# Mirror images that go from tile to tile, wider runs of u, z loaded once, and a list that reckons transfers by packets

## The chip, the core and the metric

The kernel runs on one core of a Trainium2 chip. Its time is the device time of one execution in microseconds (us). Three runs of the kernel before gave 1464.86 to 1466.71 us, median 1465.71. One more execution was recorded by the hardware profiler; the durations below come from it.

## What is computed

```python
# u, v: (2, 3008, 256); z: (2, 3008, 64)
attn = np.maximum(z @ z.T / S, 0.0) ** 2          # per batch, S = 3008
x    = u * (attn @ v)                             # 6016 tokens x 256
g    = s * np.maximum(x @ w_in1, 0) ** 2 + b      # 256 -> 2048
y    = g @ w_out1                                 # 2048 -> 256
h    = y @ w_in2
out  = (h / (1 + np.exp(-1.702 * h))) @ w_out2
```

The scores are `z @ z.T` with the same z on both sides, so the matrix of scores is symmetric: the block of keys kc and queries c is the mirror image of the block of keys c and queries kc. The weights come as 64-bit floats.

## The kernel before, in words

**Attention.** A batch's 3008 tokens are cut into six chunks, 0 to 5, of 512 tokens (one of 448). For each pair of chunks kc <= c and each of four 128-key steps t, a `Fresh` step (L434) makes scores on TensorE, then on ScalarE a relu, a square and a rounding to fp32r (`hi`); VectorE takes the rest (`lo`), and `add_up` (L412) multiplies v by hi and lo into `accA`. Where kc < c, `turn` (L485) lets VectorE transpose the squared scores in 32x32 blocks into a tile T (128 x 2048, 1 MiB). [...] `park` (L530) writes T to a buffer H in HBM by one DMA (two where c is 5), and `fetch` (L550) reads H into a tile R by four DMAs of 256 KB (six where c is 5), one for each 32 partitions. Later a `Turned` step (L574) casts R to hi (L593, ScalarE), takes lo (L597, VectorE) and multiplies into `accB`. Each batch has fifteen such images. A step's matmuls stand five steps (`LAG`) behind its casts in the list.

**u, z, v.** When a chunk's sum is complete, `gate` (L904) loads u for it with `load_u` (L869): two halves of four DMAs of 64 KB each, in runs of 32 floats (128 bytes), and transposes and multiplies. `load_z` (L306) loads each chunk of z twice, into the lower and the upper 64 partitions, in runs of 128 bytes. `split_v` (L397) splits v into high and low parts.

**Weights and the two layers.** Weights are read as 64-bit words, turned to fp32 on VectorE and ScalarE (`decode`, L645), combined and split (`prepare`, L703) and stored in HBM. This "preparation" is spread over attention (layer 0) and over attention and the first layer (layer 1). The layers multiply pairs of token blocks by eight quads of weights with seven or eight products each; their loads of prepared weights are issued as tiles come free.

**What sets the order.** All work is first put in a list of `Op`s with an engine, a cost and the keys it reads and writes. `ordered` (L25) takes TensorE's list as written (it may reach 16 ahead) and simulates the engines to place everything else; it models the transfers as one pipe at 350 KB per us (`rate`) and never gives a tile out before its pool has one. Pools: 58 cells of 2 KB per partition, 14 "big" of 4 KB, 4 "wide" of 8 KB (T, R and the `up` weights). The program is then emitted in that order. Each engine runs its instructions in order, so a transfer on SyncE's queue (SP) waits behind all issued before it, and a cast of R on ScalarE that waits holds up all of ScalarE.

Of the kernel before, what the change touches and what calls it, by code (L numbers as in the profile page):

```python
# [14 lines left out]
class Op:  # L15


    def __init__(self, engine, cost, late, f, reads, writes, new, adds, free, due, kb, soon):
        self.engine, self.cost, self.late, self.f = engine, cost, late, f
        self.reads, self.writes, self.new, self.adds = list(reads), list(writes), list(new), list(adds)  # L20
        self.free, self.due, self.kb, self.soon = free, due, kb, soon
        self.keys = set(self.reads) | set(self.writes) | set(self.adds)


def ordered(ops, counts, clocks, reach, ahead, bulk, spread, rate):  # L25
# [116 lines left out]
    while len(result) < n:  # L142
# [43 lines left out]
        for j in after[i]:  # L186
            waiting[j] -= 1
            ready[j] = max(ready[j], s0 + (lag(i, j) if not op.kb else op.cost + late))
            if not waiting[j] and ops[j].engine != "PE":
                pending[ops[j].engine].append(j)  # L190
# [4 lines left out]
def attention_mlp_mlp_kernel(  # L195
# [35 lines left out]
    COUNTS = dict(cell=58, big=14, wide=4, ps=4, accA=2, accB=2)  # L231
# [41 lines left out]
    def put(engine, cost, late, f, reads=(), writes=(), new=(), adds=(), free=0, due=None, kb=0, soon=None):  # L273
        ops.append(Op(engine, cost, late, f, reads, writes, new, adds, free, due, kb, soon))
# [7 lines left out]
    def move(kb, f, reads=(), writes=(), new=(), engine="SP", **more):  # L282
        put(engine, 0.45, 2.0, f, reads, writes, new, kb=kb, **more)

    def moves(kb, fs, reads=(), writes=(), new=(), engine="SP", **more):
        def f():
            for g in fs:
                g()

        put(engine, 0.45 * len(fs), 2.0, f, reads, writes, new, kb=kb, **more)  # L290
# [15 lines left out]
    def load_z(bb, t):  # L306
# [8 lines left out]
        for i in range(4):  # L315
# [15 lines left out]
        moves(64 * len(fs["SP"]), fs["SP"], (), [key], [(key, "cell")], due=due)  # L331
        if fs["ACT"]:
            moves(128, fs["ACT"], (), [(key, 1)], (), engine="ACT", due=due)
# [34 lines left out]
    def load_v(bb, c):  # L368
# [24 lines left out]
        moves(128 * len(fs["SP"]), fs["SP"], (), [key], [(key, "big")], due=due)  # L393
        if fs["ACT"]:
            moves(256, fs["ACT"], (), [(key, 1)], (), engine="ACT", due=due)

    def split_v(bb, c, t):  # L397
        raw, key = ("vr", bb, c), ("v", bb, c, t)

        def high():  # L400
            T[key] = cell(f"v_{bb}_{c}_{t}", F32R).rearrange("p (h d) -> p h d", h=2)
            nc.scalar.copy(out=T[key][:, 0, :], in_=T[raw][:, t, :])

        def low():
            w = T[key]
            nc.vector.tensor_tensor(out=w[:, 1, :], in0=T[raw][:, t, :], in1=w[:, 0, :], op=ALU.subtract)
# [166 lines left out]

    class Turned:  # L574
# [70 lines left out]
    def decode(layer, j):  # L645
# [4 lines left out]
        def load(k):  # L650
            if k == 0:
                T[key] = big_tile(f"wr_{layer}_{j}", U32)
                src = w_in[:, j * 2 * P : (j + 1) * 2 * P].rearrange("(k p) f -> p k f", p=P)
                nc.sync.dma_start(out=T[key][:, :CH].rearrange("p (k f) -> p k f", k=2), in_=src)
# [37 lines left out]
        if layer == 0:  # L692
# [8 lines left out]
            vector(HALF, add, [wf] + ([("total",)] if j else []), [("total",)], **more)  # L701

    def prepare(layer, i, with_sums):  # L703
# [64 lines left out]
        for o in range(2):  # L768
# [41 lines left out]
    def load_forms(layer, p, f, some):  # L810
# [12 lines left out]
        move(256, run, [("df", layer, f, i) for i in some], [key], [(key, "cell")])  # L823
# [45 lines left out]
    def load_u(m, h):  # L869
        start, n = tokens(m)  # L870
        key = "ur", m, h
        fs = []
        for i in range(4):

            def f(i=i):
                if key not in T:
                    T[key] = cell(f"ur_{m}_{h}").rearrange("p (t a) -> p t a", a=32)
# [8 lines left out]
        moves(256, fs, (), [key], [(key, "cell")])  # L886

    def turn_u(m, h):
        n = tokens(m)[1]
        ur, ut = ("ur", m, h), ("ut", m, h)  # L890

        def f():
            T[ut] = cell(f"ut_{m}_{h}")
            if m < 2 * LASTC:
                nc.vector.transpose(
                    out=T[ut].rearrange("p (t g a) -> p t g a", t=4, g=4),
                    in_=T[ur].rearrange("p (g t) a -> p t g a", g=4),
                )
            else:
                nc.vector.transpose(out=T[ut][:, :n], in_=T[ur][:, : n // 32, :].rearrange("p t a -> p (t a)"))  # L900

        vector(n, f, [ur], [ut], [(ut, "cell")])

    def gate(m, accs):  # L904
        n, key = tokens(m)[1], ("x", 0, m)
        for h in range(2):
            load_u(m, h)
# [51 lines left out]
    def post(layer, m, h, source, reads):  # L959
# [30 lines left out]
        for i in range(4):  # L990
# [14 lines left out]
            move(64, f, [key], (), (), engine=queue)  # L1005
# [406 lines left out]
    steps = []  # L1412
    groups = [(0, (1, 2, 3)), (1, (2, 3, 4)), (2, (3, 4)), (3, (4,)), (0, (4, 5)), (1, (5,)), (2, (5,)), (3, (5,)), (4, (5,))]
# [12 lines left out]
    def write_list():  # L1426
# [9 lines left out]
        for k in range(len(steps) + LAG):  # L1436
            if k < len(steps):
# [6 lines left out]
                elif t == 0:  # L1444
# [88 lines left out]
        [(20.0, 450.0), (200.0, 800.0)], 350.0,  # L1533
# [45 lines left out]
```

## Time and profile before

| | |
|---|---|
| the profiled execution | 1461.43 us, of which the span is 1459.7 |
| median of the runs | 1465.71 us |
| TensorE busy | 1398.3 us (96%), 6147 matmuls |
| VectorE busy | 1315.0 us (90%) |
| ScalarE busy | 1210.6 us (83%) |
| DMA | 280956 packets, 326.81 MB; 138448 of them under 512 bytes |
| attention | up to about 540 us; after it the two layers |

The rows further down are groups of whole lines. "Busy" is the time in which an engine executes; a matmul takes 0.23 us of TensorE when it runs at full rate. PEclk is the granted clock as a share of full speed; DMA share is the mean busy share of the 16 DMA engines. A number in brackets at a row's end is the idle time of the engine ahead of the instruction, and what ended it. SPq is the queue of DMA issues on SyncE.

### The profile page before, as it was taken

How to read it: one execution, taken by the hardware profiler on the slowest of the kernel's cores; microseconds unless marked ns; L12 is line 12 of the kernel's file. 1: busy time of each engine (PE TensorE's matmuls, PEld its weight loads, DVE VectorE, ACT ScalarE, POOL GpSimd, SP SyncE). 2: the span in 40 equal slices, each digit the busy share in tenths (PEclk: the TensorE clock that was granted, in tenths of full speed). 3: DMA queues.
4: the chain of work that ended last, by engine and by line, in shares of the span. 5: the costliest groups of instructions: out<-in, count | busy, mean ns of one | idle time of the engine just before them, and what ended most of it. 6: DMA issues, size and time to landing. Idle time of an engine off the chain costs nothing.

```text
span 1459.7 us, 20185 instructions
## 1 busy us (share of the span) xinstructions
PE 1398.3 (96%) x6147; PEld 1157.0 (79%) x6147; DVE 1315.0 (90%) x2368; ACT 1210.6 (83%) x2360; POOL 3.0 (0%) x10
## 2 busy tenths in 40 slices
PE   8999897998989879999999999999999999999997
PEld 6877786777878668888887888898888888888896
DVE  7989897788989769999999999989999999999996
ACT  8988786788878559898999989897979797978784
POOL 0000000000000000000000000000000000000000
PEclk9999999999999999999999999999999999999999
DMA  6788999969699988666786847575756665666654
GB/s 160 229 224 262 256 237 205 273 209 248 230 273 262 225 280 278 214 219 223 256 279 203 295 174 242 168 267 168 270 157 240 182 234 162 243 190 228 190 190 108
DMA packets 280956, 326.81 MB, mean 224 GB/s; under 512 B 138448, under 2 KB 210640, under 8 KB 278288
## 3 DMA queue, kind: packets, MB, share of 16 engines
q1 hardware_dynamic: 277056, 324.62, 72.7%
q10 hardware_dynamic: 3664, 0.68, 0.3%
q8 instruction: 48, 0.79, 0.2%
q14 instruction: 60, 0.49, 0.1%
q0 software_dynamic: 128, 0.23, 0.1%
HBM read 245.24 MB, written 80.22 MB: 223 GB/s over the span
## 4 chain that ended last, share of the span: by engine, by line
PE 72%; DMA 9%; DVE 8%; ACT 4%; SPq 4%; issue 2%; ACTq 0%; POOL 0%; DVEq 0%; POOLq 0%
PE ps_d L1048 8%; PE ps_b L1048 8%; PE ps_c L1048 8%; PE accB L1241 7%; PE ps_b L1241 5%; PE ps_a L1048 4%; PE ps_d L1241 4%; DMA R<-H 4%; PE ps_c L1241 3%; PE accA L1241 3%; PE accA L1216 3%; PE accB L1216 3%; PE accA L427 2%; PE accA L422 2%; PE accB L422 2%; PE accA L423 2%
## 5 line engine op out<-in xcount | busy, mean ns | idle before, releaser
L1171 DVE TENSOR_TENSOR lo<-g_c,hi 128x512 fp32r<-128x512 f32 (+1 forms) x540 | 346.8, 678 | 12.3 <-ACT hi L1167 11.7
L1167 ACT CAST hi<-g_c 128x512 fp32r<-128x512 f32 (+1 forms) x540 | 310.5, 617 | 4.1 <-DVE g_c L1156 3.0
L422 PE MATMUL accA<-hi,v 128*128 128x512 f32 (+1 forms) x336 | 132.5, 394 | 8.3 <-ACT hi L462 6.1
L423 PE MATMUL accA<-hi,v 128*128 128x512 f32 (+1 forms) x336 | 130.7, 389 | 0.0
L1048 PE MATMUL ps_d<-op_t,up 128*128 128x512 f32 (+1 forms) x432 | 120.8, 388 | 2.1 <-DVE g_c L1122 1.9
L1048 PE MATMUL ps_b<-op_t,up 128*128 128x512 f32 (+1 forms) x432 | 121.1, 389 | 0.2 <-ACT s_u L1097 0.2
L593 ACT CAST hi<-R 128x512 fp32r<-128x512 f32 x120 | 70.2, 622 | 59.6 <-DMA R<-H 58.5
L422 PE MATMUL accB<-hi,v 128*128 128x512 f32 x240 | 96.4, 402 | 18.8 <-ACT hi L593 18.8
L466 DVE TENSOR_TENSOR lo<-a,hi 128x512 fp32r<-128x512 f32 (+1 forms) x166 | 109.1, 662 | 4.2 <-ACT hi L462 3.8
L1134 ACT ACTIVATE g_c<-g_c 128x512 f32<-128x512 f32 (+1 forms) x144 | 89.6, 623 | 27.9 <-DVE g_c L1122 27.6
L1156 DVE TENSOR_TENSOR g_c<-g_c,g_c 128x512 f32<-128x512 f32 (+1 forms) x156 | 105.7, 677 | 1.5
L455 ACT ACTIVATE a<-ps_s 128x512 f32<-128x512 f32 (+1 forms) x168 | 96.0, 584 | 13.3 <-PE ps_s L451 13.0
L451 PE MATMUL ps_s<-zq,zk 128*128 128x512 f32 (+1 forms) x336 | 98.9, 388 | 8.4 <-ACT a L455 6.4
L427 PE MATMUL accA<-lo,v 128*128 128x512 f32 (+1 forms) x332 | 102.4, 390 | 4.4 <-DVE lo L466 4.4
L458 ACT ACTIVATE a<-a 128x512 f32<-128x512 f32 (+1 forms) x168 | 103.4, 627 | 0.7
L462 ACT CAST hi<-a 128x512 fp32r<-128x512 f32 (+1 forms) x168 | 101.3, 613 | 0.4
L597 DVE TENSOR_TENSOR lo<-R,hi 128x512 fp32r<-128x512 f32 x110 | 71.5, 677 | 30.8 <-ACT hi L593 26.7
L1048 PEld LDWEIGHTS ps_d<-op_t,up 128*128 128x128 f32 x432 | 80.3, 188 | 20.0 <-DVE g_c L1122 4.3
L423 PE MATMUL accB<-hi,v 128*128 128x512 f32 x240 | 95.5, 398 | 0.0
L1241 PE MATMUL accB<-hi,d 128*128 128x512 f32 (+1 forms) x312 | 95.1, 386 | 0.0
L1048 PEld LDWEIGHTS ps_b<-op_t,up 128*128 128x128 f32 x432 | 80.9, 189 | 17.0 <-ACT s_u L1097 0.9
L1137 ACT ACTIVATE g_c<-g_c 128x512 f32<-128x512 f32 (+1 forms) x144 | 88.2, 631 | 0.4
(167 smaller groups left out, 3320.3 us busy)
## 6 DMA issues: line engine op xcount, KB each, us to landing
up<-uf SPq DMA_DIRECT2D x96, 896.0 KB, 4.8
d<-dw SPq DMA_DIRECT2D x114, 256.0 KB, 4.9
R<-H SPq DMA_DIRECT2D x100, 256.0 KB, 6.6
H<-T SPq DMA_DIRECT2D x20, 1024.0 KB, 5.3
d_s<-df1s SPq DMA_DIRECT2D x54, 256.0 KB, 5.8
f<-rows SPq DMA_DIRECT2D x20, 512.0 KB, 6.8
d_s<-df0s SPq DMA_DIRECT2D x72, 128.0 KB, 5.2
d_s<-df0s SPq DMA_DIRECT2D x36, 256.0 KB, 6.0
```

Source lines behind the costliest of these rows:

```text
L422: nc.tensor.matmul(T[k][:, :n], w[:, 0, cols], T[hi][:, :n], **start_flags(k, fresh))
L423: nc.tensor.matmul(T[k][:, :n], w[:, 1, cols], T[hi][:, :n], **start_flags(k, ()))
L427: nc.tensor.matmul(T[k][:, :n], w[:, 0, cols], T[lo][:, :n], **start_flags(k, ()))
L451: nc.tensor.matmul(T[self.p][:, :n], k, T[zq][:, h, :n], start=h == 0, stop=h == 1)
L458: nc.scalar.activation(out=T[self.a][:, :n], in_=T[self.a][:, :n], func=AF.Square)
L462: nc.scalar.copy(out=T[self.hi][:, :n], in_=T[self.a][:, :n])
L466: nc.vector.tensor_tensor(out=T[self.lo][:, :n], in0=T[self.a][:, :n], in1=T[self.hi][:, :n], op=ALU.subtract)
L1048: nc.tensor.matmul(to[:, :n], a[h], y[:, g, :n], start=first and j == 0, stop=False, skip_group_check=True)
L1156: nc.vector.tensor_tensor(out=self.get(to), in0=self.get(x), in1=self.get(y), op=ALU.subtract)
L1167: nc.scalar.copy(out=T[keys[0]][:, :n], in_=self.get(c))
L1171: nc.vector.tensor_tensor(out=T[keys[1]][:, :n], in0=self.get(c), in1=T[keys[0]][:, :n], op=ALU.subtract)
L1241: nc.tensor.matmul(to[:, :n], w[:, h, cols], g[:, :n], start=first and j == 0, stop=False, skip_group_check=True)
```

## The change

`Op` carries `pipe`, the time that a transfer takes of the modelled pipe, worked out by `carry` from its bytes and the length of its runs. FAR holds the eight pairs (kc, c) with c in 1, 2 and 5, which are parked and fetched as before; the seven with c in 3 and 4 go by `send`: sixteen DMAs of 64 KB from T to R, issued as soon as T is complete. Chunks of z other than the first two are loaded for 64 partitions and copied to the other 64 by one DMA inside SBUF. u is loaded by four DMAs of 128 KB in runs of 64 floats; that permutes the 256 columns, so v's columns and the first layer's rows of `w_in` are permuted alike. The second half of `down_whole` is stored only for quads that use it (3 and 7 in layer 0, 7 in layer 1). Pools: 56 cells, 13 big, 5 wide.

```diff
-    COUNTS = dict(cell=58, big=14, wide=4, ps=4, accA=2, accB=2)
+    COUNTS = dict(cell=56, big=13, wide=5, ps=4, accA=2, accB=2)
...
-        if op.kb:
-            pipe = max(pipe, s0 + op.cost) + op.kb / rate
+        if op.pipe:
+            pipe = max(pipe, s0 + op.cost) + op.pipe
...
+    def carry(kb, run):
+        return kb * 1024 / run * (0.0185 + run / 27200) / 16
...
-        for i in range(4):
+        twice = bb == 0 and t < 2
+        for i in range(4 if twice else 2):
...
+        if not twice:
+            move(128, lambda: nc.sync.dma_start(out=T[key][64:], in_=T[key][:64]), [key], [key])
...
-            nc.scalar.copy(out=T[key][:, 0, :], in_=T[raw][:, t, :])
+            nc.scalar.copy(out=permuted(T[key][:, 0, :], "(h i a)"), in_=permuted(T[raw][:, t, :], "(i h a)"))
...
+    def send(bb, kc, c):
...
+        for x in range(4):
+            for g in range(4):
+                def f(x=x, g=g):
+                    src = T[key].rearrange("p b s r -> p b (s r)")[32 * g : 32 * g + 32, x]
+                    nc.sync.dma_start(out=tile_of()[32 * x : 32 * x + 32, g], in_=src)
+                fs.append(f)
+        moves(1024, fs, [key], [to], [(to, "wide")], soon=0.5)
...
-        for o in range(2):
+        for o in range(1 if i in always[layer] else 2):
             store(256, key, ("dw", layer, i, o), lambda to, o=o: nc.sync.dma_start(
...
-    def load_u(m, h):
+    def load_u(m, due):
...
-                    in_=u.rearrange("b s d -> (b s) d")[
-                        start : start + n, h * P + 32 * i : h * P + 32 * i + 32
-                    ].rearrange("(t b) a -> b t a", b=32),
+                    in_=u.rearrange("b s d -> (b s) d")[start : start + n, 64 * i : 64 * i + 64].rearrange(
+                        "(t b) a -> b t a", b=32
+                    ),
...
-        moves(256, fs, (), [key], [(key, "cell")])
+        moves(512, fs, (), [key], [(key, "big")], run=256, due=due)
...
+    FAR = [(kc, c) for c in (1, 2, LASTC) for kc in range(c)]
...
-                    park(bb, kc, c)
+                    (park if (kc, c) in FAR else send)(bb, kc, c)
```

Three places on SyncE's queue show what the new list does. In names, the tile's kind stands first and the last number is a running number; R_1_4 is the image of chunks 1 and 4, ur is u, zr is z, vr is v, H the parked image.

In the second batch, where chunk 4's images are made, this stood before:

```order
L541 DMA H_2_4_4523<-T_2_4_4441 128x2048
L569 DMA R_1_4_4550<-H_1_4_4420 32x4x512 x4
L781 DMA df0s_108<-forms_6_3_4561 128x2x128
L781 DMA df0s_109<-forms_6_3_4561 128x2x128
L781 DMA df0s_110<-forms_6_3_4561 128x2x128
L781 DMA df0s_111<-forms_6_3_4561 128x2x128
L541 DMA H_3_4_4619<-T_3_4_4538 128x2048
L569 DMA R_2_4_4637<-H_2_4_4523 32x4x512 x4
```

At the same place on SyncE's queue stands now:

```order
L601 DMA R_0_4_4299<-T_0_4_4237 32x512 x16
L601 DMA R_1_4_4430<-T_1_4_4372 32x512 x16
L330 DMA zr_5_4547<-in_z_dram 32x14x32
L330 DMA zr_5_4547<-in_z_dram 32x2x32
L330 DMA zr_5_4547<-in_z_dram 32x14x32
L330 DMA zr_5_4547<-in_z_dram 32x2x32
L340 DMA zr_5_4547<-zr_5_4547 64x512
L601 DMA R_2_4_4661<-T_2_4_4463 32x512 x16
```

A write of H and a later fetch behind other transfers became one run of sixteen pieces for each image.

Where chunk 3's images are made in the second batch, SyncE's queue now reads:

```order
L601 DMA R_0_3_3789<-T_0_3_3704 32x512 x16
L601 DMA R_1_3_3877<-T_1_3_3819 32x512 x16
L330 DMA zr_4_3977<-in_z_dram 32x16x32 x2
L601 DMA R_2_3_3986<-T_2_3_3908 32x512 x16
L340 DMA zr_4_3977<-zr_4_3977 64x512
L582 DMA R_1_2_4084<-H_1_2_3575 32x4x512 x4
```

Three sends of 48 pieces now stand right ahead of the fetch of the image of chunks 1 and 2; that fetch stood ahead of all of chunk 3's transfers but one write.

At the end of the second batch's attention, ahead of the last fetch (chunks 4 and 5), SyncE's queue had:

```order
L878 DMA ur_0_5555<-in_u_dram 32x16x32 x4
L878 DMA ur_1_5575<-in_u_dram 32x16x32 x4
L781 DMA df1s_115<-forms_3_3_5313 128x2x128
L781 DMA df1s_116<-forms_3_3_5313 128x2x128
L541 DMA H_4_5_5609<-T_4_5_5483 128x1024
L541 DMA H_4_5_5609<-T_4_5_5483 128x2x384
L790 DMA up_0_1_5627<-uf_76 128x1792
L878 DMA ur_0_5633<-in_u_dram 32x14x32 x4
L820 DMA d_0_s_0_5659<-df0s_111 128x256
L858 DMA rows_5_129<-gx_5562 128x1024
L878 DMA ur_0_5670<-in_u_dram 32x16x32 x4
L569 DMA R_4_5_5697<-H_4_5_5609 32x4x512 x2
```

Now it has there:

```order
L554 DMA H_4_5_5606<-T_4_5_5485 128x1024
L554 DMA H_4_5_5606<-T_4_5_5485 128x2x384
L904 DMA f_0_5618<-rows_0_123 128x1024
L904 DMA f_1_5628<-rows_1_124 128x1024
L808 DMA dw_98<-forms_7_2_5466 128x2x256 x2
L917 DMA ur_5643<-in_u_dram 32x16x64 x4
L829 DMA up_0_1_5670<-uf_76 128x1792
L859 DMA d_0_s_0_5680<-df0s_111 128x256
L842 DMA d_0_0_0_5695<-dw_91 128x512
L582 DMA R_4_5_5727<-H_4_5_5606 32x4x512 x2
```

Sixteen issues of u around the last image became four; the rest of u stands earlier, or behind the fetch, and two loads of the first layer's operands (f) moved in.

## Rows read from the trace of the kernel before

**Rows 1.** Busy time by stretch; the first line names the columns; stretches of each phase

```profile
core 0: us, PE busy (x) PEld busy (x) DVE busy (x) ACT busy (x) POOL busy (x), PEclk, DMA share, GB/s
0.00:540.00 540.00, 490.56 (x2104) 400.69 (x2105) 454.77 (x918) 425.64 (x851) 0.34 (x6) 0.96 0.87 238
600.00:850.00 250.00, 249.00 (x1089) 203.25 (x1088) 247.36 (x429) 228.90 (x437) 0.00 (x0) 1.00 0.68 231
850.00:900.00 50.00, 49.92 (x220) 40.65 (x219) 44.64 (x73) 46.13 (x89) 0.00 (x0) 1.00 0.61 211
1200.00:1250.00 50.00, 50.00 (x221) 41.12 (x220) 47.33 (x79) 38.74 (x73) 0.00 (x0) 1.00 0.70 215
```

**Rows 2.** The same view of attention's stretches where TensorE falls behind

```profile
0.00:20.00 20.00, 14.49 (x54) 8.80 (x55) 12.17 (x25) 15.26 (x30) 0.34 (x6) 1.00 0.76 171
140.00:160.00 20.00, 13.31 (x52) 10.14 (x51) 14.96 (x26) 13.48 (x27) 0.00 (x0) 0.83 1.01 268
230.00:260.00 30.00, 22.13 (x83) 16.37 (x83) 24.47 (x49) 22.49 (x46) 0.00 (x0) 0.89 0.93 240
270.00:280.00 10.00, 8.86 (x37) 6.40 (x36) 5.93 (x12) 8.24 (x16) 0.00 (x0) 1.00 0.85 252
290.00:300.00 10.00, 4.66 (x12) 3.26 (x13) 6.37 (x12) 7.32 (x15) 0.00 (x0) 0.71 0.55 151
350.00:360.00 10.00, 5.20 (x16) 3.71 (x16) 7.17 (x14) 5.72 (x12) 0.00 (x0) 0.83 1.03 278
410.00:420.00 10.00, 6.10 (x22) 4.76 (x21) 6.22 (x12) 6.53 (x13) 0.00 (x0) 0.83 1.08 300
480.00:530.00 50.00, 38.17 (x150) 30.29 (x149) 35.44 (x68) 26.57 (x52) 0.00 (x0) 0.86 0.98 265
```

**Rows 3.** Who waited for whom: total us, times, longest us

```profile
ACT hi L593 <- DMA R<-H: 58.5, 13, 7.2
PE accB L422 <- ACT hi L593: 18.8, 4, 6.5
```

**Rows 4.** Timeline of ScalarE: start, length, casts of R that waited for it

```profile
150.70 0.62 ACT L593 CAST hi<-R 128x512 fp32r<-128x512 f32 x1 [6.52 <-DMA R<-H]
...
248.50 1.66 ACT L593 CAST hi<-R 128x512 fp32r<-128x512 f32 x3 [3.76 <-DMA R<-H]
...
292.68 0.62 ACT L593 CAST hi<-R 128x512 fp32r<-128x512 f32 x1 [5.49 <-DMA R<-H]
...
355.38 2.18 ACT L593 CAST hi<-R 128x512 fp32r<-128x512 f32 x4 [4.25 <-DMA R<-H]
...
413.47 1.66 ACT L593 CAST hi<-R 128x512 fp32r<-128x512 f32 x3 [5.05 <-DMA R<-H]
...
517.27 2.18 ACT L593 CAST hi<-R 128x512 fp32r<-128x512 f32 x4 [7.16 <-DMA R<-H]
```

**Rows 5.** DMA issues: count, KB each, median us from issue to landing

```profile
R<-H SPq DMA_DIRECT2D x100, 256.0 KB, 6.6
H<-T SPq DMA_DIRECT2D x20, 1024.0 KB, 5.3
...
ur<-in_u_dram SPq DMA_DIRECT2D x80, 64.0 KB, 2.7
```

**Rows 6.** Length of one issue on SyncE, ns min/median/max, fetches and u

```profile
L569 SPq DMA_DIRECT2D R<-H x140: 302/431/3325, 30.5 to 512.3; - x140
...
L878 SPq DMA_DIRECT2D ur<-in_u_dram x96: 311/487/2129, 193.5 to 533.0; - x96
```

**Rows 7.** Timeline of SyncE's queue: two of the loads of u late in attention

```profile
471.81 6.98 SPq L878 DMA_DIRECT2D ur<-in_u_dram  x8
...
481.11 4.68 SPq L878 DMA_DIRECT2D ur<-in_u_dram  x8
```

**Rows 8.** DMA queues: packets, MB, share of 16 engines' span; the queue of small packets

```profile
q10 hardware_dynamic: 3664, 0.68, 0.3%
```

**Rows 9.** One instruction of the preparation on VectorE, ns min/median/max

```profile
L673 DVE SCALAR_TENSOR_TENSOR mt<-wr,mt x32: 648/688/700, 15.4 to 788.9; 128x512 f32<-128x512 uint32 x32
```

More of the change, by code (lines that the diff above doesn't have):

```diff
@@ L15, with __init__, ordered @@
 class Op:
-    def __init__(self, engine, cost, late, f, reads, writes, new, adds, free, due, kb, soon):
+    def __init__(self, engine, cost, late, f, reads, writes, new, adds, free, due, pipe, soon):
         self.engine, self.cost, self.late, self.f = engine, cost, late, f
         self.reads, self.writes, self.new, self.adds = list(reads), list(writes), list(new), list(adds)
-        self.free, self.due, self.kb, self.soon = free, due, kb, soon
+        self.free, self.due, self.pipe, self.soon = free, due, pipe, soon
         self.keys = set(self.reads) | set(self.writes) | set(self.adds)
-def ordered(ops, counts, clocks, reach, ahead, bulk, spread, rate):
+def ordered(ops, counts, clocks, reach, ahead, bulk, spread):
     n = len(ops)
@@ L271, in attention_mlp_mlp_kernel, with put @@
     ops, T = [], {}
-    def put(engine, cost, late, f, reads=(), writes=(), new=(), adds=(), free=0, due=None, kb=0, soon=None):
-        ops.append(Op(engine, cost, late, f, reads, writes, new, adds, free, due, kb, soon))
+    def put(engine, cost, late, f, reads=(), writes=(), new=(), adds=(), free=0, due=None, pipe=0, soon=None):
+        ops.append(Op(engine, cost, late, f, reads, writes, new, adds, free, due, pipe, soon))
     def scalar(n, f, reads=(), writes=(), new=(), **more):
@@ L280, in vector, with move, moves @@
         put("DVE", 0.065 + (0.00056 if fast else 0.00105) * n, 0.14, f, reads, writes, new, **more)
-    def move(kb, f, reads=(), writes=(), new=(), engine="SP", **more):
-        put(engine, 0.45, 2.0, f, reads, writes, new, kb=kb, **more)
-    def moves(kb, fs, reads=(), writes=(), new=(), engine="SP", **more):
+    def carry(kb, run):
+        return kb * 1024 / run * (0.0185 + run / 27200) / 16
+    def move(kb, f, reads=(), writes=(), new=(), engine="SP", run=2048, **more):
+        put(engine, 0.45, 2.0, f, reads, writes, new, pipe=carry(kb, run), **more)
+    def moves(kb, fs, reads=(), writes=(), new=(), engine="SP", run=2048, **more):
         def f():
@@ L288, in f @@
                 g()
-        put(engine, 0.45 * len(fs), 2.0, f, reads, writes, new, kb=kb, **more)
+        put(engine, 0.45 * len(fs), 2.0, f, reads, writes, new, pipe=carry(kb, run), **more)
     def matmuls(count, n, f, reads=(), adds=(), writes=(), new=()):
@@ L392, in load_v, with permuted @@
         due = 0.5 if (bb, c) == (0, 0) else None
-        moves(128 * len(fs["SP"]), fs["SP"], (), [key], [(key, "big")], due=due)
+        moves(128 * len(fs["SP"]), fs["SP"], (), [key], [(key, "big")], run=1024, due=due)
         if fs["ACT"]:
-            moves(256, fs["ACT"], (), [(key, 1)], (), engine="ACT", due=due)
+            moves(256, fs["ACT"], (), [(key, 1)], (), engine="ACT", run=1024, due=due)
+    def permuted(x, order):
+        return x.rearrange(f"p {order} -> p h i a", h=2, i=4)
     def split_v(bb, c, t):
@@ L652, in load @@
                 T[key] = big_tile(f"wr_{layer}_{j}", U32)
-                src = w_in[:, j * 2 * P : (j + 1) * 2 * P].rearrange("(k p) f -> p k f", p=P)
-                nc.sync.dma_start(out=T[key][:, :CH].rearrange("p (k f) -> p k f", k=2), in_=src)
+                to, src = T[key][:, :CH].rearrange("p (k f) -> p k f", k=2), w_in[:, j * 2 * P : (j + 1) * 2 * P]
+                if layer:
+                    nc.sync.dma_start(out=to, in_=src.rearrange("(k p) f -> p k f", p=P))
+                    return
+                for h in range(2):
+                    half = src.rearrange("(i h a) f -> h i a f", i=4, h=2)[h]
+                    nc.sync.dma_start(out=to[:, h], in_=half)
             else:
@@ L701, in decode @@
             vector(HALF, add, [wf] + ([("total",)] if j else []), [("total",)], **more)
+    always = [set(range(NQ)).intersection(*[SEVEN.get((layer, p), ()) for p in range(NP)]) for layer in range(2)]
     def prepare(layer, i, with_sums):
@@ L821, in run @@
                 T[key, i] = t[:, y].rearrange("p (h n) -> p h n", h=2)
-        move(256, run, [("df", layer, f, i) for i in some], [key], [(key, "cell")])
+        move(128 * len(some), run, [("df", layer, f, i) for i in some], [key], [(key, "cell")], run=1024)
         for i in some:
@@ L1003, in f @@
                 )
-            move(64, f, [key], (), (), engine=queue)
+            move(64, f, [key], (), (), engine=queue, run=128)
     form_key = {}
```

39 lines of the change are left out of this document (27 added, 12 removed).

## The prediction

> **What bounds the kernel now.** I read the busy time by stretches first. After 600 us TensorE is busy for 249.0 of 250 us and later for all of 50, at a granted clock of 1.00 [rows 1]: the two layers run at TensorE's rate, and nothing that this change does can shorten them. In the 540 us before, TensorE starts 2104 matmuls. At the rate of the later stretch (221 in 50 us, 4.42 per us, 0.226 us each) it could start 2387. The 283 that are missing are 64 us: all that can be won lies there, and the kernel keeps some 1396 us whatever is done.
>
> Next I cut attention finely. The missing matmuls sit in a few stretches [rows 2]: 4.42 times the length, less the matmuls started, times 0.226 us. The start, 0 to 20: 34, 7.8 us. 140 to 160: 36, 8.2 us. 230 to 260: 50, 11.2. 270 to 280: 7, 1.6. 290 to 300: 32, 7.3. 350 to 360: 28, 6.4. 410 to 420: 22, 5.0. 480 to 530: 71, 16.1. Without the start that is 55.8 us. Each price holds the idle time and the slow clock behind it: the granted clock is 0.71 to 0.89 in those stretches whose TensorE stood longest, and 1.00 in the layers [rows 1, 2].
>
> Then who waits. ScalarE waited 13 times, 58.5 us in total, for a transfer from H to R, and TensorE then for ScalarE's cast of R [rows 3]. The timeline puts these waits at the stretches above: 6.5 us ahead of 150.7, 3.8 ahead of 248.5, 5.5 ahead of 292.7, 4.3 ahead of 355.4, 5.1 ahead of 413.5, 7.2 ahead of 517.3 [rows 4]. By SyncE's order the casts at 150.7, 355.4 and 413.5 are of images (1,4) of the first batch, (0,3) and (1,4) of the second; all three go by send now. The casts at 248.5, 292.7 and 517.3 are of (4,5) of the first batch, (0,1) and (4,5) of the second; these are parked and fetched as before. The DMA engines are 87% busy over attention and at 0.93 to 1.08 in most of the bad stretches [rows 1, 2]: the images are late because the pipe and SyncE's queue are full.
>
> **Sends.** An image was a write (5.3 us to landing), then four fetches (6.6 us each, issued 0.43 us apart), with other transfers between [rows 5, 6]: 5.3 + 4 x 0.43 + 6.6 = 13.6 us with nothing between. Now it is sixteen pieces of 64 KB. The trace has no copy from SBUF to SBUF. Below, 16 x 0.43 + 2.7 (the landing of a 64 KB load of u) = 9.6 us; above, at the price of u under load (8 in 6.98 us, 0.87 each [rows 7]), 16 x 0.87 + 2.7 = 16.6 us. I take 9.6 to 11, nearest to the fetch, whose runs are as long (2 KB) where u's are 128 bytes. The room for it I counted in ScalarE's order, from the square of an image's last step to the first cast of R; one ScalarE instruction passes each 0.63 us in attention (540 / 851 [rows 1]). The three images above have 31, 29 and 30 instructions now (37, 40 and 40 before): 18 us, of which the transposition takes some 3. So 15 us hold 9.6 to 11, and hold nearly the upper bound. I give these stretches back for 85%: 0.85 x 19.6 = 16.7 us.
>
> **Less on the pipe.** Fourteen sends save one megabyte each, 14.7 MB. Attention moves 238 GB/s at 87% busy, 274 GB/s of full pipe, so that is 54 us of it. u keeps its bytes and has 24,064 packets instead of 48,128, z 14,336 instead of 24,576. A small packet costs up to 19 ns of an engine: 0.3% of 16 x 1459.7 us over 3664 [rows 8]; below, nothing, if only bytes counted. So up to 34,304 x 19 ns / 16 = 41 us more. Together 54 to 95 of 470 busy us.
>
> **The end of attention, 480 to 530.** u's bursts go (two of eight issues took SyncE 7.0 and 4.7 us [rows 7]), and of the sixteen issues around the last image four are left. The room of the last four images, (1,5) to (4,5), grows from 38, 29, 27 and 28 instructions to 42, 40, 38 and 38: ten more are 6.3 us, against a longest wait of 7.2 [rows 4]. But f and prepared weights, some 3.3 MB by the shapes in the order against 2.0, now stand between the last write and its fetch. I take 75%: 12 us of 16.1.
>
> **230 to 260.** Images (3,5) and (4,5) of the first batch have 29 and 34 instructions for 26 and 32: one or two us more, against waits of up to 4.5. u and z around them halve their issues. Half: 5.5 of 11.2.
>
> **270 to 300.** The room of (0,1) stays at 39. The eight loads of u right ahead of its write go, the write of weights among them stays. Half: 4.5 of 8.9.
>
> **What is added.** Issues: a send has sixteen for five, u four for eight, z three for four; SyncE gets about 90 more, 39 us at 0.43 [rows 6], in a queue that waits much. Where three sends stand together and the fetch of (1,2) right behind them, 48 issues take 20.6 us or more; that fetch has about 93 to 99 instructions of room from its square, but only a few from its own issue. Between nothing (LAG covers five steps of TensorE) and a full wait of 7 us in each batch; I take 2 each, 4 in all. Preparation: by VectorE's order two more of the 64-bit blocks (five instructions each), 5 more splits and 8 more sums of layer 1 now stand behind attention. These 23 are at most 0.69 us each [rows 9], 15.9 us; the splits and sums cover 128 to 512 columns where that one covers 512, so I take 10. VectorE is busy for 247 of 250 us in the first layer up to 850 and 44.6 of 50 behind [rows 1]. TensorE lost 1 us there with one quad of weights for each pair of blocks, and now a fourth pair gets one: 1 us, between 0 (44.6 + 5 still fits) and 5 (half of it late). The permuted copies of v, the strided transposes of u, the split load of `w_in` and the smaller pools keep elements and instructions nearly as they were; 0, within 1 us either way, behind ScalarE's and VectorE's idle time in attention. The start keeps its 7.8 us.
>
> **The sum.** 16.7 + 12 + 5.5 + 4.5 - 4 - 1 = 33.7 us less. The profiled execution took 1461.4 (a span of 1459.7 and 1.7 around it), so 1427.7 for its like; the median of the runs lies 4.3 above it, which gives 1432.
>
> **Rivals.** First, the fetched images stay as late as they are: six of the sixteen remaining fetches have the room they had, to within two instructions, and the pipe is still some 75% busy. Only the sends' 16.7 us less 5 come: 1454. For it speaks that a fetch with room for 39 instructions was late by 5.5 us at 292.7, when the DMA share was only 0.55 [rows 2, 4], so fullness of the pipe isn't all. Against it, the room grows by ten at the end. Second, nearly everything goes: 55.8 less 4, 1414. For it, late images are the cause of most waits [rows 3]; against it, VectorE is busy for 455 of 540 us [rows 1] and has less slack in 505. Third, slower: SyncE's queue becomes what is late. Its place is the sends of chunks 3 and 4, its price the piece. At 0.43 us the 224 pieces take 96 us of the queue; each 0.1 us more adds 22. If half of that shows (five of seven sends have short room, and hold up what stands behind them), the gain of 33.7 is gone at 0.30 more, so it decides from 0.73 us a piece. At u's 0.87 the half is 49 us, and the time 1481. u's rows under a full pipe say 0.59 to 0.87 [rows 7]; against it, u's runs are 128 bytes. The Trainium skill (SBUF — State Buffer, Can I just issue two DMAs to hit both halves?) has a rule against this change: two concurrent DMAs, on tiles at partition 0 and at 64, gained 6% over one, so they serialize. Pieces that follow one another at the landing of u's would take 16 x 2.7 = 43 us a send. The trace speaks against it: eight issues of u pass in 4.68 us with a landing of 2.7 each, so several are under way at once [rows 5, 7]. Fourth, images come in time and TensorE waits for VectorE or `up` weights instead: no change, 1465.
>
> **How the numbers follow.** The forecast has 52%, the first and the second rival 17% each, the third 8%, the fourth 6%. Faster (by over 0.2%, 3 us, about what a measurement of this kernel can tell from none): 86%. Same: 6%. Slower: 8%. The forecast's own range, with sends at 50 to 100% and the fetches at 30 to 80% of their losses, is 1422 to 1450 (20.7 to 48.6 us won, less 5). For 8 times in 10 it must take in the second rival and the first: 1410 to 1462.
>
> **What would show it.** In the new profile ScalarE's waits for transfers from T to R should be under 5 us in total, those from H to R about 20. An issue of a send should last 0.4 to 0.5 us. 480 to 530, shifted by what was won before, should start over 200 matmuls. The DMA share of attention should be near 0.76, packets some 36,000 fewer. The stretch of the first layer should stay within 2 us of TensorE's rate. I'm wrong if sends last over 12 us, if the fetch of (1,2) makes TensorE wait over 4 us in a batch, or if attention ends at the same time with the images in time.

## The result and the profile after

The changed kernel takes 1475.7 us (median of 4 runs, 1472.7 to 1477.2), the kernel before 1465.3 beside it: the ratio is 1.0067, 95% interval 1.005 to 1.0085. It is slower by 0.7%, where 1432 us and a gain were forecast. The profiled execution took 1477.2 us, its span is 1475.4.

I start with the windows. Columns as in [rows 1, 2]: busy us and, in brackets, instructions of TensorE, its weight loads, VectorE, ScalarE and GpSimd; then the granted clock, the DMA share and GB/s. First the kernel before, cut at 560 us, by which attention is over, in two stretches in which it had lost next to nothing, and in two whose rows are wanted below:

```profile
0.00:560.00 560.00, 509.18 (x2185) 415.26 (x2186) 473.89 (x952) 443.24 (x885) 0.34 (x6) 0.96 0.86 239
560.00:1459.70 899.70, 889.14 (x3964) 741.78 (x3962) 841.12 (x1416) 767.32 (x1476) 2.63 (x4) 1.00 0.66 215
100.00:120.00 20.00, 19.52 (x86) 16.15 (x87) 19.93 (x46) 15.22 (x30) 0.00 (x0) 1.00 0.60 191
360.00:390.00 30.00, 30.00 (x134) 24.83 (x133) 27.45 (x59) 25.11 (x50) 0.00 (x0) 1.00 0.50 169
...
270.00:300.00 30.00, 23.28 (x91) 17.40 (x90) 22.00 (x42) 22.75 (x46) 0.00 (x0) 0.90 0.77 216
530.00:550.00 20.00, 18.72 (x83) 15.15 (x82) 16.09 (x27) 15.36 (x29) 0.00 (x0) 1.00 0.76 252
```

The same of the changed kernel, with the stretches of [rows 2] behind them:

```profile
0.00:560.00 560.00, 508.12 (x2133) 411.01 (x2134) 449.82 (x904) 431.64 (x857) 0.34 (x6) 0.95 0.72 197
560.00:1475.40 915.40, 903.58 (x4016) 748.25 (x4014) 862.79 (x1465) 782.22 (x1504) 2.62 (x4) 1.00 0.67 217
100.00:120.00 20.00, 11.05 (x32) 7.73 (x31) 8.96 (x16) 6.20 (x13) 0.00 (x0) 0.66 0.78 203
360.00:390.00 30.00, 18.65 (x69) 14.05 (x68) 12.92 (x22) 14.60 (x29) 0.00 (x0) 0.77 0.75 187
...
140.00:160.00 20.00, 15.59 (x66) 12.31 (x65) 13.62 (x26) 13.38 (x29) 0.00 (x0) 0.93 0.64 188
230.00:260.00 30.00, 27.88 (x123) 21.84 (x122) 27.13 (x53) 22.57 (x46) 0.00 (x0) 1.00 0.99 252
270.00:300.00 30.00, 30.00 (x127) 24.64 (x126) 25.10 (x47) 28.29 (x58) 0.00 (x0) 0.95 0.76 228
350.00:360.00 10.00, 10.00 (x46) 8.29 (x45) 8.10 (x16) 9.46 (x20) 0.00 (x0) 1.00 0.39 94
410.00:420.00 10.00, 10.00 (x46) 8.29 (x45) 9.11 (x21) 10.00 (x22) 0.00 (x0) 1.00 0.42 99
480.00:530.00 50.00, 46.23 (x199) 39.32 (x200) 47.33 (x99) 40.23 (x80) 0.00 (x0) 0.93 1.04 292
530.00:550.00 20.00, 15.90 (x59) 11.74 (x58) 12.26 (x20) 10.72 (x20) 0.00 (x0) 0.91 1.05 317
```

By 560 us TensorE has started 52 matmuls fewer: 52 x 0.227 = 11.8 us. Behind it 4016 matmuls take 915.4 us, where the rate of before (3964 in 899.7) would take 911.5: 3.9 us. Together that is the 15.7 us between the spans. The old bad stretches of [rows 2] start 193 matmuls more than before. New bad ones have come; the two largest are 100 to 120 and 360 to 390, with 54 and 65 matmuls fewer, 27 us, and in them the granted clock is 0.66 and 0.77, where it was 1.00.

They are not the whole loss. In a kernel that runs behind or ahead, a window by the clock holds other work than before, so the same place in the work has to be compared too. Each trace has 6147 matmuls of TensorE; the table sets the start of the n-th beside that of the n-th before (the two orders differ by a few places), both counted from the first matmul. The last column is of a run below.

| matmul | starts before at, us from the span's start | the change lags by, us | send_4_same_order lags by, us |
|---|---|---|---|
| 100 | 30.5 | 2.6 | 2.4 |
| 400 | 101.5 | -0.4 | -0.7 |
| 450 | 112.9 | 12.7 | -0.7 |
| 550 | 135.6 | 12.7 | -0.7 |
| 600 | 155.5 | 11.4 | -9.4 |
| 700 | 177.4 | 11.4 | -9.4 |
| 950 | 231.3 | 16.6 | -9.5 |
| 1000 | 251.2 | 10.9 | -17.8 |
| 1050 | 265.4 | 15.2 | -14.2 |
| 1200 | 309.7 | 4.8 | -24.6 |
| 1350 | 343.7 | 6.9 | -23.6 |
| 1400 | 361.6 | 0.3 | -30.2 |
| 1450 | 373.0 | 15.2 | -30.2 |
| 1600 | 407.0 | 15.2 | -30.2 |
| 1650 | 423.8 | 10.3 | -35.6 |
| 1750 | 445.6 | 10.3 | -35.7 |
| 1850 | 466.9 | 22.4 | -35.7 |
| 2050 | 527.8 | 6.5 | -48.5 |
| 2100 | 539.1 | 13.4 | -41.1 |
| 2250 | 574.9 | 11.4 | -43.1 |
| last | 1450.3 | 15.4 | -38.8 |

The two large stretches lose 13.1 us (matmuls 400 to 450) and 14.9 (1400 to 1450) by this count. Two others lose 5.2 (700 to 950) and 12.1 (1750 to 1850), and smaller ones 4.3 (1000 to 1050) and 6.9 (2050 to 2100).

The timeline of SyncE's queue (start, length, line, instruction, count) shows what stands at the two largest, and two sends between them:

```profile
72.00 10.65 SPq L601 DMA_DIRECT2D R<-T  x16
82.75 1.09 SPq L330 DMA_DIRECT2D zr<-in_z_dram  x2
83.94 21.49 SPq L601 DMA_DIRECT2D R<-T  x32
105.47 0.59 SPq L340 DMA_DIRECT2D zr<-zr  x1
106.16 1.97 SPq L582 DMA_DIRECT2D R<-H  x4
...
143.02 12.12 SPq L601 DMA_DIRECT2D R<-T  x16
...
179.90 10.01 SPq L601 DMA_DIRECT2D R<-T  x16
...
362.21 10.01 SPq L601 DMA_DIRECT2D R<-T  x16
372.27 0.59 SPq L340 DMA_DIRECT2D zr<-zr  x1
372.90 2.02 SPq L582 DMA_DIRECT2D R<-H  x4
```

From 72 to 105 us SyncE issues almost nothing but the 48 pieces of three sends, 0.63 to 0.67 us each. Behind them stand the copy of chunk 4's z (L340) and the fetch of the image of (1,2); the expectations below call an image a half. The timelines of the engines that want them (the idle time before, and its releaser, in brackets):

```profile
107.85 0.71 DVE L348 STREAM_TRANSPOSE zt<-zr 128x512 f32<-128x512 f32 x1 [9.16 <-DMA zr<-zr]
...
109.52 0.80 PE L464 MATMUL ps_s<-zq,zk 128*128 128x512 f32 x1 [6.44 <-DVE zq L361]
...
113.80 2.18 ACT L625 CAST hi<-R 128x512 fp32r<-128x512 f32 x4 [13.83 <-DMA R<-H]
...
156.81 0.62 ACT L625 CAST hi<-R 128x512 fp32r<-128x512 f32 x1 [6.62 <-DMA R<-T]
...
191.42 0.62 ACT L625 CAST hi<-R 128x512 fp32r<-128x512 f32 x1 [7.30 <-DMA R<-T]
```

Waits up to 560 us (total, times, longest), against [rows 3]:

```profile
ACT hi L625 <- DMA R<-H: 40.8, 8, 15.3
DVE zt L348 <- DMA zr<-zr: 22.7, 4, 9.2
ACT hi L625 <- DMA R<-T: 20.8, 6, 7.3
PE ps_s L464 <- DVE zq L361: 15.1, 3, 8.0
```

The casts' waits, 40.8 us for fetched images and 20.8 for sent ones, come to 61.6 us, for 58.5 before.

And the length of one issue in ns (min/median/max), against [rows 6]:

```profile
L601 SPq DMA_DIRECT2D R<-T x224: 507/589/1906, 72.0 to 448.7; - x112
...
L582 SPq DMA_DIRECT2D R<-H x84: 302/430/1682, 33.4 to 526.2; - x84
```

### The profile page after: what moved, and what is told of

Read it like the earlier page. It is cut to its first block, busy times and chain, and to the rows that moved or that the text cites. A ratio compares the mean times of both kernels' runs of the same rounds, so it can differ in the third digit from the quotient of the medians.

```text
span 1475.4 us, 20284 instructions
## 1 busy us (share of the span) xinstructions
PE 1411.7 (96%) x6147; PEld 1159.3 (79%) x6147; DVE 1312.6 (89%) x2368; ACT 1213.9 (82%) x2360; POOL 3.0 (0%) x10
## 2 busy tenths in 40 slices
DMA packets 243309, 308.73 MB, mean 209 GB/s; under 512 B 105280, under 2 KB 174144, under 8 KB 242432
## 4 chain that ended last, share of the span: by engine, by line
PE 56%; DMA 15%; DVE 11%; SPq 9%; ACT 7%; issue 3%; ACTq 0%; POOL 0%; DVEq 0%; POOLq 0%
PE ps_b L1093 8%; PE ps_d L1093 8%; PE ps_c L1093 8%; SPq L601 7%; PE accB L1286 6%; PE ps_d L1286 4%; PE ps_a L1093 4%; PE ps_b L1286 4%; DMA wr<-in_moe_w_out_dram 4%; DMA R<-H 3%; PE accA L1286 3%; PE ps_c L1286 3%; PE accA L1261 2%; DVE lo L1216 2%; PE accB L1261 2%
## 5 line engine op out<-in xcount | busy, mean ns | idle before, releaser
L625 ACT CAST hi<-R 128x512 fp32r<-128x512 f32 x120 | 70.2, 619 | 67.4 <-DMA R<-H 40.8
L464 PE MATMUL ps_s<-zq,zk 128*128 128x512 f32 (+1 forms) x336 | 105.2, 401 | 17.5 <-DVE zq L361 15.1
L479 DVE TENSOR_TENSOR lo<-a,hi 128x512 fp32r<-128x512 f32 (+1 forms) x166 | 108.5, 657 | 13.1 <-ACT hi L475 12.6
L1179 ACT ACTIVATE g_c<-g_c 128x512 f32<-128x512 f32 (+1 forms) x144 | 89.4, 621 | 32.8 <-DVE g_c L1167 32.5
L440 PE MATMUL accA<-lo,v 128*128 128x512 f32 (+1 forms) x332 | 105.1, 399 | 10.9 <-DVE lo L479 10.9
L464 PEld LDWEIGHTS ps_s<-zq,zk 128*128 128x128 f32 x336 | 65.6, 197 | 34.4 <-DVE zq L361 15.3
```

What stands on the lines that cost most here:

```text
L440: nc.tensor.matmul(T[k][:, :n], w[:, 0, cols], T[lo][:, :n], **start_flags(k, ()))
L464: nc.tensor.matmul(T[self.p][:, :n], k, T[zq][:, h, :n], start=h == 0, stop=h == 1)
L479: nc.vector.tensor_tensor(out=T[self.lo][:, :n], in0=T[self.a][:, :n], in1=T[self.hi][:, :n], op=ALU.subtract)
```

## The experiments

My theory after this: SyncE's queue works in order, a piece takes 0.6 to 0.7 us of it, and what stands behind the sends comes late. Rivals: A, the copy of z in itself; B, the list's new order and prices; C, the transfer from tile to tile in itself. Ratios are to the kernel before (1460 to 1463 us beside these runs); differences between kernels that were measured at different times are taken from the ratios, 0.1% being 1.46 us.

**The parts of the change, taken away or moved one by one**

```diff
 z_twice:    -twice = bb == 0 and t < 2
             +twice = True
 piece_price: the list's price of a sent piece 0.45 -> 0.65
 no_sends:   -FAR = [(kc, c) for c in (1, 2, LASTC) for kc in range(c)]
             +FAR = [(kc, c) for c in range(1, NCH) for kc in range(c)]
 sends_pool: in send(), nc.sync.dma_start -> nc.gpsimd.dma_start, engine="POOL"
```

> All of z is loaded twice from memory, so no half of it is copied from tile to tile; the sends stay as they are. Theory (the sends fill SyncE's queue at 0.6 to 0.7 us a piece, and whatever stands behind them is late, above all chunk 4's z copy and the fetch of the half of (1,2)): zt's longest waits for z (9.2 us, twice) fall under 2 us, but the casts still wait some 13 to 15 us for the half of (1,2), so that the windows 100 to 120 and 360 to 380 gain only some 3 to 5 us each; 1464 to 1471 us. Rival A (the copy of z by itself, a second transfer in series, is what was lost): both windows fill, and the time falls by 20 us or more, under 1456. Rival B (the list's new order and prices, whatever is moved): no change, 1473 to 1478.

Measured 1481.8 us, 1.0131 (1.0102 to 1.0159). Slower than the change by some 9 us, which none of the three expected. Rival A falls: without any copy, three sends still stand ahead of the fetch of (1,2), and in the first batch TensorE waits 9.4 us for its cast, at 113.4. So the late fetch alone is enough there.

> Only the list's price of a sent piece is changed, from 0.45 to 0.65 us, which is near what SyncE takes for one; the instructions are the same, their order is made anew. Theory: the list now sees the queue as it is, puts the copy of z and the fetch of (1,2) ahead of some of the pieces or sends later; the waits of 9 us for z and of 14 to 15 us for the half of (1,2) become less than half, 1455 to 1466 us. Rival A: as far as the copy of z comes earlier the same, else nothing. Rival C (the transfer from tile to tile is slow in itself, not its issue): the images sent are as late as before and the time stays at 1470 to 1480.

Measured 1481.2 us, 1.0128 (1.0111 to 1.0146). My theory's number was wrong: told the price, the list put 48 pieces in one run of 31.7 us instead of moving anything past them. By its number rival C (1470 to 1480) came nearest, but since the new order did not let anything past the pieces, that neither helps nor hurts it.

> All fifteen halves are written to memory and fetched back, as in the kernel before; longer runs of u, the single load of z and the list's reckoning by packets stay. Theory (the sends are what is lost): no queue of 48 pieces, the copy of z lands in time, and the time is that of the kernel before or a little under it, 1458 to 1467 us. Rival A (the copy of z in itself): still 1470 or more, with zt waiting some 9 us for z. Rival B (the list's order and prices): 1470 or more, with z in time but images late at other places.

Measured 1434.9 us, 0.9812 (0.9792 to 0.9833). Without the sends the rest of the change gains 28 us on the kernel before, more than the theory expected (1458 to 1467 us); the sends cost 2.55%, 37 us. The copy of chunk 4's z goes out at 84.98 instead of 105.47, and the fetch behind it does not stand behind pieces:

```profile
84.98 0.53 SPq L340 DMA_DIRECT2D zr<-zr  x1
...
87.45 2.69 SPq L582 DMA_DIRECT2D R<-H  x4
```

> The 224 pieces are issued by GpSimd on its own queue instead of SyncE's, and the list reckons them there. Theory (SyncE's queue is what delays the copy of z and the fetch of (1,2)): SyncE is free, z's waits fall under 3 us and those for the half of (1,2) under 6 us, 1445 to 1462 us, unless GpSimd takes far longer for a piece than SyncE does. Rival C (the transfer from tile to tile is slow in itself): casts wait for the images sent as much as now or more (20.8 us in all now), 1470 or more. Rival A: as far as the copy of z comes early, some 20 us.

Measured 1446.9 us, 0.9892 (0.9876 to 0.9907): 26 us better than the change, as the theory has it, but 12 worse than no sends. The casts still wait 21.5 us for the images sent, as much as in the change (20.8), which the expectation had named as rival C's sign; what went is the wait for z and for (1,2). A piece takes GpSimd 0.496 us (median of 224), and then VectorE waits to write the next T until the old one is sent:

```profile
DVE T L508 <- DMA R<-T: 22.0, 4, 7.1
```

**From the kernel without sends: pieces, u, z, prices**

```diff
 fetch_16:      the seven halves' fetch, per 32 rows x 4 groups -> per 32 rows x 1 group
 ns_u_narrow:   load_u, turn_u, split_v and the load of w_in as in the kernel before
 ns_z_twice:    twice = True
 ns_flat_price: -return kb * 1024 / run * (0.0185 + run / 27200) / 16
                +return kb / 350.0
```

> From no_sends (all halves by memory, 1434.9 us): the seven halves that the change sends are fetched from memory in 16 pieces of 64 KB instead of 4 of 256 KB, same bytes, same packets of 2 KB, 168 more instructions on SyncE's queue, which the list prices at 0.45 us as it does a sent piece. Theory (the number of instructions on SyncE's in-order queue is the loss): 168 x 0.43 us = 72 us more of the queue, in runs of 7 us beside the copy of z and the next fetches; at least a third of the 41 us that the sends cost comes back, 1448 to 1476 us. Rival C (the transfer from tile to tile is the loss): the same as no_sends, 1432 to 1440.

Measured 1461.0 us, 0.9987 (0.9972 to 1.0003), 26 us slower than no_sends without any image sent from tile to tile. Against rival C; but the order is new too, so the 26 us are not yet the price of the instructions alone.

> From no_sends: u is again loaded in runs of 128 bytes by halves into small tiles, without permuted columns of v and w_in. It tells what of the 28 us that no_sends gains on the kernel before is u's. By packets: 16,384 more packets of some 0.023 us over 16 engines, some 24 us of the pipe in an attention whose DMA share is 0.9 already. Theory (pipe relief by u and z is the gain): 1445 to 1458 us. Rival (the list's reckoning by packets is the gain): 1432 to 1440.

Measured 1446.4 us, 0.9884 (0.9863 to 0.9906), 11 us slower than no_sends. The packets are 24,961 more (267,596 for 242,635), not 16,384.

> From no_sends: all of z loaded twice from memory again, no copy from tile to tile. Some 18,000 more packets of 128 bytes, some 26 us of the pipe, against one copy in series for each chunk. Theory (pipe relief): slower by 3 to 15 us, 1438 to 1450. Rival A (the copy in series costs something everywhere): faster, 1425 to 1433.

Measured 1420.7 us, 0.9704 (0.9684 to 0.9725): 16 us faster than no_sends, on the side of rival A, and 43 us faster than the kernel before. It is the fastest of all runs. The packets are 9,825 more (252,460), not 18,000, so the theory's 26 us of the pipe were nearly twice too many.

> From no_sends: the list reckons a transfer again by its size alone (1 us for 350 KB) instead of by packets; the transfers are the same, only their order is made with the old price. Theory (pipe relief is the gain, the reckoning little): within 6 us of no_sends, 1429 to 1441. Rival (the reckoning is the gain): 1450 or more.

Measured 1455.8 us, 0.9948 (0.9931 to 0.9966): 20 us slower, as the rival expected (1450 or more).

**Is the reckoning a gain of its own, and how much is mere order?**

```diff
 before_packets: the kernel before, +carry()'s reckoning with each transfer's run length
 z_on_pool:      the change, the copy zr<-zr by nc.gpsimd on its queue
 sends_pool_zt:  sends_pool and z_twice together
 ns_zt_nudge, after_nudge, before_nudge:
                 the list's price of each issue 0.45 -> 0.46
```

> The kernel before with one thing changed: its list reckons a transfer by its packets (packets of 0.0185 us + run length / 27,200, over 16 engines) instead of by size. No transfer changes, only the order. Theory (ns_flat_price lost 21 us, so the reckoning is worth about that much by itself): 1438 to 1452 us. Rival (the reckoning helps only with the shorter pipe of wide u and single z): 1456 or more.

Measured 1443.5 us, 0.9888 (0.9873 to 0.9903): 16 us faster than the kernel before.

> The changed kernel with the copy of z from tile to tile issued by GpSimd, whose queue is empty, instead of by SyncE behind the sends. Theory (two losses of 12.5 and 14.4 us begin where chunk 4's copy stands behind up to three sends, but the fetch of the half of (1,2) stands there too and stays late): zt's waits of 9.2 us go, casts wait as now (40.8 us), and 4 to 16 us come back, 1459 to 1472. If the copy alone decided (rival A), 20 us or more come back, under 1456.

Measured 1467.9 us, 1.0053 (1.0037 to 1.007). Some 2 us better than the change by the ratios, which their intervals do not tell from none, and less than I expected; the list placed two loads of z and the fetch of (1,2) behind the pieces again.

> The sends issued by GpSimd, and all z loaded twice without a copy from tile to tile: every other part of the change as it is. It shows what sends are worth once SyncE's queue is spared, against the same kernel without sends (1420.7 us). Theory (a send of 16 pieces on any one queue takes 8 to 10 us and lands later than the park and fetch that it replaces): slower than that, 1425 to 1447 us. Rival (sends are good where the queue is free, since they spare a way to memory and back): 1405 to 1420.

Measured 1436.7 us, 0.984 (0.9825 to 0.9854): 20 us slower than ns_z_twice, as the theory has it.

> A control: the kernel without sends and without the copy of z (1420.7 us), in which the list prices each issue at 0.46 instead of 0.45 us. Nothing else changes but what order follows from that. How far the time moves is how far a mere change of order moves it: 1415 to 1430 us if the differences of 11 us and more between these kernels come from what was changed in them; 1435 or more if they are the order's luck.

Measured 1434.6 us, 0.9826 (0.9811 to 0.984): 18 us slower than ns_z_twice from a change of order alone, practically at the bound that I had set for luck. So the 11 us of u, the 16 us of z and the 12 us between sends_pool and no_sends can't be told from it; the 16 and 20 us of the reckoning and the 20 us of sends_pool_zt hardly, and sends_pool_zt lies within 2 us of this control.

**The same order, another number of instructions**

That left open whether 37 us, and the 26 of fetch_16, were order too. In the next two every engine's order stays as it is, and the number of pieces into which a transfer is cut changes.

```diff
 send_4_same_order, from the change; the list still reckons 16 pieces:
-  for x in range(4):
-      for g in range(4):
-          ... [32 * g : 32 * g + 32, x]  ->  tile_of()[32 * x : 32 * x + 32, g]
+  for x in range(4):
+      ... [32 * x : 32 * x + 32]  ->  tile_of()[32 * x : 32 * x + 32]
 fetch_16_same_order, from no_sends: as fetch_16; the list still reckons 4 pieces
```

> The changed kernel with every engine's work in exactly the changed kernel's order, but each send is 4 pieces of 256 KB instead of 16 of 64 KB: same bytes from tile to tile, 168 instructions fewer on SyncE's queue. It leaves out that the blocks change places, so what it sends is not the mirror image. Theory (the number of instructions on the in-order queue is the loss): a send takes some 2 us of the queue instead of 10, chunk 4's copy of z and the half of (1,2) come in time, and 20 to 40 of the 41 us come back, 1436 to 1456 us. Rival C (the transfer from tile to tile, or when it lands): 1466 or more. Rival (the list's order with sends in it is simply bad): 1460 or more too, with SyncE free.

Measured 1422.6 us, 0.9731 (0.9702 to 0.9759): 3.4% or 49 us faster than the change, more than I expected. SyncE's queue, the casts' waits for fetched images and the window up to 560 us:

```profile
71.65 3.37 SPq L600 DMA_DIRECT2D R<-T  x4
75.13 2.25 SPq L330 DMA_DIRECT2D zr<-in_z_dram  x2
78.05 10.76 SPq L600 DMA_DIRECT2D R<-T  x8
88.86 1.12 SPq L340 DMA_DIRECT2D zr<-zr  x1
90.07 2.50 SPq L582 DMA_DIRECT2D R<-H  x4
```

```profile
ACT hi L624 <- DMA R<-H: 10.8, 7, 4.4
```

```profile
0.00:560.00 560.00, 543.81 (x2375) 448.32 (x2376) 502.69 (x996) 483.43 (x956) 0.34 (x6) 0.98 0.82 225
```

The copy of z goes out 16.6 us earlier, the casts' waits for fetched images fall from 40.8 to 10.8 us, and 242 more matmuls start by 560 us. In the table above the change's four largest losses, 45.3 us together, are gone (matmuls 400 to 450, 700 to 950, 1400 to 1450, 1750 to 1850). The small ones at the start, from 1000 to 1050 and from 2050 to 2100 stay, so the sixteen pieces did not make them. The transfers are still from tile to tile, still a megabyte each: rival C falls, and with it rival B, since the order is the changed kernel's own. One thing differs besides the count: a piece's runs are 8 KB long here, not 2, so part of the 49 us may belong to that.

> The kernel without sends (1434.9 us) with every engine's work in exactly its order, but the seven halves fetched in 16 pieces instead of 4 (the list still reckons 4). Theory: 168 instructions of some 0.42 us, 70 us of the queue, cost 10 us or more without any change of order, 1445 to 1475 us. Rival (the 26 us that the 16 pieces cost before were the luck of a new order): 1432 to 1441.

Measured 1474.8 us, 1.009 (1.0056 to 1.0124), 2.8% or 41 us slower than no_sends. Here bytes and runs are the same, so this is the cleanest of the runs: 168 instructions more bring 2690 packets (242,635 to 245,325, some 16 each, nearly all under 512 bytes) and 0.02 MB. Its waits look like the change's, z's too, and two images' fetches hold SyncE for 16 us:

```profile
ACT hi L627 <- DMA R<-H: 43.1, 11, 10.3
...
DVE zt L353 <- DMA zr<-zr: 12.7, 2, 6.4
```

```profile
349.29 16.18 SPq L584 DMA_DIRECT2D R<-H  x32
...
365.98 0.52 SPq L340 DMA_DIRECT2D zr<-zr  x1
```

With each matmul set beside the same one of no_sends, all of the 41 us are lost within attention.

> A control: the changed kernel, in which the list prices each issue at 0.46 instead of 0.45 us. The work is the same, its order is made anew. If the loss against the kernel before belongs to the sends, 1465 to 1485 us; if it was one unlucky order, under 1455.

Measured 1474.0 us, 1.0081 (1.0052 to 1.011): the loss is not one unlucky order. With z_twice, piece_price and z_on_pool, five orders with the pieces on SyncE's queue lie at 1.0053 to 1.0131; three with neither sends nor sixteen pieces and with wide u and the reckoning by packets at 0.9704 to 0.9826.

> A control: the kernel before, in which the list prices each issue at 0.46 instead of 0.45 us. Order alone moved a kernel without sends by 14 us; so I expect within 15 us of the kernel before, 1446 to 1476. Outside that, the comparison of before and after says little about the change.

Measured 1458.3 us, 0.9965 (0.995 to 0.998): 5 us, inside what I expected. The kernel before is not one lucky order.

## Why the prediction was wrong

The step that failed most is "What is added". It said: "SyncE gets about 90 more, 39 us at 0.43 [rows 6], in a queue that waits much", "48 issues take 20.6 us or more", and then "I take 2 each, 4 in all". Measured: the 48 pieces and two loads of z took 33.4 us (72.00 to 105.43), and the two stretches behind such runs cost 28 us, not 4 (27 by the clock). Two errors made that. The piece was sized by the fetch, 0.43 us, and takes 0.589 at the median and 0.67 in a run. And I counted only the fetch of (1,2) as waiting behind the sends, with 93 to 99 instructions of room; the second thing there, chunk 4's copy of z, had no term in the sum at all. It is on TensorE's path by zt and zq: 15.1 us of its waits, up to 8.0 each. For the cast of (1,2) TensorE waited only 2.1 and 3.0 us more behind that; but z_twice shows that the fetch alone would have held it as long.

The second step that failed is "Sends", by the same wrong price. Together the two make 45 of the 49 us between the forecast (33.7 us less) and the result (15.7 more): 24 by "What is added", 21 by "Sends". send_4_same_order shows that cutting a send into sixteen made both. Step by step, by the table of matmuls:

- Sends: their three stretches gained 1.3, 6.6 and 4.9 us (matmuls 550 to 600, 1350 to 1400, 1600 to 1650), 12.8 for 16.7. But 17.3 us were lost in two places that had no term, 700 to 950 and 1750 to 1850, and with four pieces a send both losses are gone. By the order in which chunk 4's images are sent, the late ones in the first batch are (1,4), one of the three whose room I had counted, and (3,4), whose room I had not: the casts wait 6.6 us at 156.8, where (1,4) had waited 6.5 before, and 7.3 at 191.4. From the first issue to the cast these took 13.8 and 11.5 us, for "9.6 to 11"; the issue alone is 10.0 to 12.1. In the second batch two casts wait 2.7 and 3.4 us (437.7 and 450.8). Casts wait 20.8 us for sends in all, for "under 5".
- Less on the pipe: right. 280,956 packets became 243,309, 37,647 fewer for "some 36,000", and the DMA share up to 560 us fell from 0.86 to 0.72, for 0.76. That it did not help says that the pipe was not what was late: no_sends has 0.87 up to 560 us and is 37 us faster, and in the sends the share is 0.39 to 0.42 at 94 to 99 GB/s (350 to 360, 410 to 420). A piece of 64 KB each 0.67 us is 98 GB/s; with the pipe under half busy, I take it that the queue sets that rate.
- The end of attention: about as forecast, 15.9 us (1850 to 2050) for 12, though part of that makes good what 1750 to 1850 had lost. Just behind it, 2050 to 2100, 6.9 us are lost. send_4_same_order loses 7.4 there, so the sixteen pieces did not make it, and the cause stays open.
- 230 to 260 and 270 to 300: 11.8 us (950 to 1200) for 10.
- The layers: 4.0 us (2250 to the last) for 1, within the 0 to 5 given. VectorE is busy 862.8 of 915.4 us behind 560 us, for 841.1 of 899.7; that more of the preparation fell behind attention than I had counted would explain it, and is not shown.
- The smaller things, "0, within 1 us": not settled. u's narrow loads cost 11 us in one order, the single load of z 16 in another, and order alone 18. The list's reckoning by packets, which I gave no term, came out at 16 and 20 us in two comparisons. No more can be said of the parts' own sizes.

The third rival had the mechanism, the place and nearly the time (1481 for 1475.7), and I gave it 8%. That the time lay so near is partly luck: it was worked out for 0.87 us a piece, and at 0.67 the same rule gives 27 us, 1459. I set its threshold at 0.73 us a piece, reckoning that half of a longer issue would show. Runs at 0.67 already sufficed, since in fetch_16_same_order even a median of 0.42 us a piece costs 41 us: what matters, as I read it, is that 16 instructions stand in a row ahead of others, not their last tenth. I let "nearest to the fetch" decide a price whose upper bound held the whole sign.

The first rival's reason, that fetched images stay late, came true in another place. Of the rule that I weighed, that two transfers at once only serialize, the traces say the same as before: in sends_pool a piece lands 3.6 us after its issue (median of 224) and the next is issued 0.50 us later, so several are under way at once.

The Trainium skill (SBUF — State Buffer, The DMA setup-cost knee) has the rule that I should have weighed instead: join transfers into the largest single one, since a loop of 64 KiB tiles runs at some 30% of the rate of a single transfer of 4 MiB. It lays that to a fixed time per transfer that is mostly completion. Here the rate in the sends is 94 to 99 GB/s beside 292 in a full stretch, a third; but pieces do not wait for one another's completion, and the runs with the same order speak for the count on the issuing queue.

## What to carry to other kernels

Count a queue's instructions, not only its bytes: a transfer that is cut into sixteen pieces spares the pipe and blocks an in-order queue for 10 us, and everything behind it, even the smallest copy, waits. Before such a change, list what stands right behind the new instructions and who needs it; that list held the two largest losses here. Afterwards compare the same work and not only the same stretch of time: the other two large losses show only so. And where a scheduler makes the order anew, run a nudge of one of its prices beside the change, or keep the order and change one thing: order alone moved this kernel by up to 18 us, more than most parts of the change.

## What the runs showed that I had not expected

A piece of 64 KB from tile to tile takes SyncE 0.589 us to issue at the median, a fetch of 256 KB from memory 0.430, and in fetch_16_same_order, where 224 fetches are of 64 KB and 84 larger, the median is 0.420. A piece of 256 KB from tile to tile takes 0.634, and in the row of eight at 78.05 in send_4_same_order 1.35. So the size counts for little at the median and for more in a row: there four times the bytes took twice the time, and three sends passed in 17 us (71.65 to 88.81) instead of 33. GpSimd takes 0.496 for the same piece. Each DMA instruction more on SyncE's queue added some 16 small packets. With only 4 pieces of longer runs a send from tile to tile was as good as the way through memory: 1422.6 us beside 1420.7 to 1434.9 without sends, in other orders. A send of four pieces that also makes the blocks change places, as the kernel needs, was not run.
